# Attention, a transform and a channel-mixing layer on one core: three weight conversions in flight instead of two, and a weight block loaded earlier

## The chip, the cores and the metric

One core of one Trainium2 chip. The metric is the device time of one execution in microseconds; the figure shown is the median of three runs. A profiled execution is a run of its own, and its trace has a span from the first to the last instruction.

## The reference, cut to what matters

Four batches, eight heads, 1152 keys of 64 values; queries are averaged in pairs, which leaves 576 per head.

```
q_pool = q.reshape(B, H, S // 2, 2, D).mean(axis=3)
attn = softmax(q_pool @ k.T / sqrt(D));  x = attn @ v            # -> (4, 576, 512)
u = x + real(fft(fft(x, axis=1), axis=2))
un = (u - mean(u)) / sqrt(var(u) + 1e-6)
out = u + maximum(un @ w_ch1, 0) @ w_ch2                          # 512 -> 2048 -> 512
```

The two weight matrices come as 64-bit floats, and the kernel turns them into pairs of 32-bit floats (a high and a low part) on the chip.

## The kernel before, in words

**Attention.** The 32 heads are taken in 16 pairs, each in five units of query rows, 80 units in all. A unit has score matmuls (`s_piece`, L216) with a scaled copy and running minimum on DVE (L218), the exponential on ACT (L230), transposes on PE in `t_step` (L243) whose copies to SBUF go mostly to ACT (L246), and the product with the values in `av` (L259), whose result ACT copies into an output tile `x` (L263). Heads are loaded by SP and POOL's queue (L126, L127) and prepared on POOL (L185, L186, L192). The denominators go through DRAM (L279, L288) and are applied on POOL (L294).

**Per batch, beside attention.** When the four pairs of a batch are done, `mid` runs the transform (`dft`: folds on DVE, L490 and L498 on PE, additions on POOL, L503 and L504, and on DVE, L508) and the normalisation (`norm`: L522 to L590, with one matmul pair at L571). Then `ffn` does channel mixing in 32 blocks: 16 of the first matrix (`f1`: 12 matmuls, Relu on ACT at L697, the low part on DVE at L698) and 16 of the second (`f2`: 12 matmuls, an addition on DVE at L710), alternately four and four. A block needs one weight block of 512 KB, loaded by `wload` (L670) two blocks ahead into one of three buffers. Results go out at L712, from the same output tile that attention wrote.

**Conversions.** `convert` turns one raw weight block into its pair, 32 in all, numbered 0 to 31 here in the order of use, which is also that of the blocks of a batch (block 1 uses conversion 0). It loads the raw block on SP (L610, buffer `wraw`), takes an absolute value on ACT (L619), clamps and shifts on DVE (L621, L623), converts the low word on ACT (L625), merges on DVE (L629), masks on DVE (L632), copies on ACT (L636), does three steps on POOL (L637 to L639) and stores the pair to DRAM on SP (L645). `wraw` has two buffers; four tiles of the tag `cv` serve `wa`, `rest` and `wb` of all conversions in turn. The list `inside` lets one conversion at a time be between L619 and L639. Only batch 0 has to wait for conversions: its `ffn` steps past a block when the block two ahead has been stored.

**What sets the order.** There is no scheduler at work: the Python code writes every instruction down once, and each engine and queue runs its own in that order, waiting on semaphores. The code keeps a counter `now` in nanoseconds. Each step of attention adds a fixed amount, and what `convert` yields is how far `now` must come before its next step is written (the steps go through `after` and `run_events`). `conversions` starts a new one when `now` has reached `cdue` and fewer than two are running. `going` is filled when the first `ffn` begins. Between steps of attention `background` writes steps of `mid` and `ffn`. There are five output tiles; `drain`, called before unit 50 ends (the first unit of pair 10), writes steps of `ffn` of batch 0 until its block 30 is written, and no attention meanwhile, because that unit's result goes into batch 0's first tile.

Line numbers are those of the kernel before. Names in rows leave buffer numbers out.

Of the kernel before, what the change touches and what calls it, by code (L numbers as in the profile page):

```python
# [12 lines left out]
F32 = mybir.dt.float32  # L13
F32R = mybir.dt.float32r
I32 = mybir.dt.int32
# [9 lines left out]
P = 128  # L25
# [3 lines left out]
NH = HT + 1  # L29
# [25 lines left out]
def fused_kernel(ctx: ExitStack, tc: tile.TileContext, k2, q2, v2, w1, w2, cst, out):  # L55
# [10 lines left out]
    smp = pool("sm", 2)  # L66
    cvp = pool("cv", 1)
# [18 lines left out]
    def mtile(shape, dt, name):  # L86
        return mdp.tile(shape, dt, tag="mid", name=name)
# [4 lines left out]
    def ftile():  # L92
        return gtile() if tail[0] else ps_f.tile([P, 512], F32, tag="f", name="f")
# [322 lines left out]
    def dft(b):  # L416
# [3 lines left out]

        tmp = mtile([P, 2, SQ], F32, "tmp")
        last = smp.tile([1, SQ], F32, tag="last", name="last", bufs=1)
        z = smp.tile([1, NH], F32, tag="z", name="z", bufs=1)
        gap = 600 if b < B - 1 else 0
        nc.vector.tensor_copy(tmp[D:D + 1, 0, :], ua[:1, 1, :])
        nc.scalar.copy(last, ub[:1, 1, :])
# [178 lines left out]
    going = []  # L605

    def convert(f, which):
        src = (w1, w2)[which]
        w = cvp.tile([P, 512, 2], I32, tag="wraw", name="wraw", bufs=2)
        nc.sync.dma_start(w, src[f].bitcast(I32).rearrange("p (c x) -> p c x", x=2))  # L610
        yield 4000 if going else 7000
        while inside:
            yield 400
        inside.append(f)
        high, low = w[:, :, 1], w[:, :, 0]
        a = cvp.tile([P, 512], F32, tag="cv", name="wa", bufs=4)
        ai = a.bitcast(I32)

        nc.scalar.activation(a, high.bitcast(F32), AF.Abs)  # L619
        yield 1400  # L620
        nc.vector.tensor_scalar(a, a, WORD_MIN, WORD_MAX, op0=ALU.max, op1=ALU.min)  # L621
        yield 1000
        nc.vector.tensor_scalar(ai, ai, 3, 0x3FFFFFF8, op0=ALU.logical_shift_left, op1=ALU.bitwise_and)  # L623
        rest = cvp.tile([P, 512], F32, tag="cv", name="rest", bufs=4)
        nc.scalar.activation(rest, low.bitcast(U32), AF.Copy, scale=2.0 ** -52)  # L625
        yield 1000
        t = cvp.tile([P, 512], F32, tag="cv", name="wb", bufs=4)
        b = t.bitcast(I32)
        nc.vector.scalar_tensor_tensor(b, high, -0x40000000, ai, op0=ALU.bitwise_and, op1=ALU.bitwise_or)  # L629

        yield 1000
        nc.vector.tensor_scalar(ai, b, -0x800000, None, op0=ALU.bitwise_and)  # L632
        yield 1000
        h = w.rearrange("p c x -> p (c x)").rearrange("p (x c) -> p x c", x=2)
        hi, lo = h[:, 0, :], h[:, 1, :]
        nc.scalar.copy(hi.bitcast(F32R), t)  # L636
        nc.gpsimd.tensor_tensor(rest, rest, a, op=ALU.mult)  # L637
        nc.gpsimd.tensor_tensor(t, t, hi.bitcast(F32), op=ALU.subtract)
        nc.gpsimd.tensor_tensor(lo.bitcast(F32R), t, rest, op=ALU.add)  # L639
        if not going:  # L640
            yield 3000
        inside.pop()
        yield 3000 if going else 1500
        d = scw.tile([P, 2, 512], F32, name=f"w{which}_{f}")
        nc.sync.dma_start(d, h.bitcast(F32))  # L645
        wsc[which, f] = d
# [4 lines left out]
    todo = deque(ORDER)  # L651
    busy = []

    def converter():

        w, f = todo.popleft()
        g = convert(f, w)
        busy.append(f)

        def go():  # L660
            c = next(g, None)
            if c is not None:
                after(c, go)
            else:
                busy.pop()
        go()

    def wload(which, f, nm):
        w = wp.tile([P, 2, 512], F32R, tag="w", name=nm)
        nc.sync.dma_start(w.bitcast(F32), wsc[which, f])  # L670
        return w
# [5 lines left out]
    def mm3(ps, ah, al, bh, bl, first, last):  # L677
        nc.tensor.matmul(ps, lhsT=ah, rhs=bh, start=first, stop=False)  # L678
        nc.tensor.matmul(ps, lhsT=al, rhs=bh, start=False, stop=False)  # L679
        nc.tensor.matmul(ps, lhsT=ah, rhs=bl, start=False, stop=last)  # L680

    def ffn(b):
        gs = {}
        hl = u = None

        n_tok = NT if b < B - 1 else NL

        def f1(f, t, w):
            src = (gp, "g") if t == 0 else (kv, "ks")
            g = gs[f, t] = src[0].tile([P, 2, n_tok], F32R, tag=src[1], name="g" if b < B - 1 else "g3")  # L690
            w = w.rearrange("p x (j c) -> p x j c", j=4)
            hi, lo = hl[t]
            ps = ftile()[:, :n_tok]
            for j in range(4):
                mm3(ps, w[:, 0, j, :], w[:, 1, j, :], hi[j // 2][:, j % 2, :n_tok], lo[j // 2][:, j % 2, :n_tok],
                    j == 0, j == 3)
            nc.scalar.activation(g[:, 0, :], ps, AF.Relu)  # L697
            after(1000, lambda: nc.vector.scalar_tensor_tensor(g[:, 1, :], ps, 0.0, g[:, 0, :].bitcast(F32),  # L698
                                                               op0=ALU.max, op1=ALU.subtract))

        def f2(q, m, t, w):
            w = w.rearrange("p x (i c) -> p x i c", i=GF)
            ps = ftile()[:, :n_tok]
            for i in range(GF):
                g = gs[q * GF + i, t]
                mm3(ps, w[:, 0, i, :], w[:, 1, i, :], g[:, 0, :], g[:, 1, :], i == 0, i == GF - 1)
            x = u[m // 2][:, m % 2, :]
            last = q == NFC // GF - 1
            if b < B - 1:
                nc.vector.tensor_tensor(x[:, :NT], ps, x[:, :NT], op=ALU.add)  # L710
                if last:
                    after(2500, lambda: nc.sync.dma_start(out[b, m, :, :NT], x[:, :NT]))  # L712
                return
            c = slice(t * HT, t * HT + HT)
            r = rest[:, m, t * 96:t * 96 + 96]
            nc.vector.tensor_tensor(x[:, c], ps[:, :HT], x[:, c], op=ALU.add)
            nc.vector.tensor_tensor(r, ps[:, HT:], r, op=ALU.add)
            if last:
                nc.sync.dma_start(out[b, m, :, c], x[:, c])
                if t:  # L720
                    nc.sync.dma_start(out[:B - 1, m, :, NT:].rearrange("b p c -> p b c"),
                                      rest[:, m].rearrange("p (b c) -> p b c", b=B - 1))

        blocks = [(q, which, i) for q in range(NFC // GF) for which in range(2) for i in range(GF)]

        def load(n):
            at = b + n // len(blocks), n % len(blocks)
            if at[0] < B and at not in loads:
                q, which, i = blocks[at[1]]
                loads[at] = wload(which, q * GF + i, f"w{which + 1}")  # L730

        for n, (q, which, i) in enumerate(blocks):
            while b == 0 and n + 2 < len(blocks) and (blocks[n + 2][1], blocks[n + 2][0] * GF + blocks[n + 2][2]) not in wsc:
                yield 0
            if n == 0:
                load(0)
                load(1)
                yield 0
                while b not in ready:
                    yield 0  # L740
                going.append(b)
                hl = un.pop(b)
                u = ut.pop(b)
                if b == B - 1:
                    rest = mtile([P, 4, 3 * D], F32, "rest3")
                    nc.sync.dma_start(rest, left[2])
            load(n + 2)
            w = loads.pop((b, n))
            for t in range(len(hl)):
                if which == 0:  # L750
                    f1(q * GF + i, t, w)
                else:
                    f2(q, i, t, w)
                if q == NFC // GF - 1 and t == len(hl) - 1:
                    if which == 0 and i == GF - 1:
                        done_f1.add(b)
                    if which == 1:
                        done_f2.add((b, i))
                yield 2720 if b < B - 1 else 2080

    def mid(b):
        yield 0, 1000
        yield from dft(b)
        yield 0, 3500
        yield from norm(b)
        yield 0, 4500
        ready.append(b)

    now = due = credit = 0.0
    cdue = 60000.0  # L770
# [6 lines left out]
    def after(wait, fn):  # L777

        heapq.heappush(events, (now + wait, next(tick), fn))
# [55 lines left out]

    def conversions():
        nonlocal cdue
        if now >= cdue and todo and len(busy) < 2:
            converter()
            cdue = now + (5500 if going else 10000 if nb == 0 else 8500)  # L840

    nb = 0
    for pe in attention():
# [72 lines left out]
```

## Time and profile before

| | before |
|---|---|
| median of 3 runs | 1078.88 us (1074.13 to 1081.51) |
| profiled execution, its span | 1081.19 us, 1079.4 us |
| PE busy, PE weight loads | 984.8 us (91%), 853.7 us (79%) |
| DVE, ACT, POOL busy | 630.8 (58%), 525.1 (49%), 372.7 us (35%) |
| DMA | 170.89 MB, mean 158 GB/s |
| mean granted clock of PE | 0.968 |
| chain that ended last | PE 59%, DVE 8%, DMA 5%, issue 3%, ACT 3% |

The span is what the trace covers; the profiled execution's own time is 1.8 us longer. PE overlaps weight loads with matmuls, so its busy time is not all work at its peak; idle time of PE, and the granted clock of a stretch (1.00 is 2.4 GHz, 0.50 is 1.2 GHz), are read from stretches.

### The profile page before, as it was taken

The page shows a single profiled execution, that of the slowest core. Times are in us where ns is not written, and L with a number is a line of the kernel's source. Part 1 is how long each engine was busy: PE and PEld are TensorE (multiplying, and loading weights), DVE is VectorE, ACT ScalarE, POOL GpSimd, SP SyncE. Part 2 cuts the span into 40 slices and gives each one's busy share as a digit, 9 for nine tenths or more (in the row PEclk, how much of TensorE's full clock was granted, in tenths as well). Part 3 has the DMA queues.
Part 4 walks back from the last instruction along what each step waited for, and adds up shares of the span by engine and source line. Part 5 has one row for each costly group of instructions (what it writes and reads, how often), then busy time and mean ns, then how long its engine had stood idle before and what let it go on. Part 6 is the DMA issues. An engine that isn't in the chain of part 4 may idle for free.

```text
span 1079.4 us, 19451 instructions
## 1 busy us (share of the span) xinstructions
PE 984.8 (91%) x7392; PEld 853.7 (79%) x7392; DVE 630.8 (58%) x1518; ACT 525.1 (49%) x1017; POOL 372.7 (35%) x351
## 2 busy tenths in 40 slices
PE   6999998988799899994599999989899989999998
PEld 5898876767688777773488888878688867899998
DVE  5556879798576597986435457475544254522222
ACT  5678876667455466674144445455444421311100
POOL 3545666665355456664322222252200002000000
PEclk9999999999899899997799999999999999999999
DMA  5545656544566665645536355234532243634344
GB/s 180 168 133 168 201 158 207 176 130 152 163 228 228 213 210 175 203 165 180 192 131 190 129 176 137 82 107 144 164 124 91 92 153 117 216 142 135 118 127 127
DMA packets 62512, 170.89 MB, mean 158 GB/s; under 512 B 16770, under 2 KB 20242, under 8 KB 62420
## 3 DMA queue, kind: packets, MB, share of 16 engines
q1 hardware_dynamic: 58100, 151.96, 44.1%
q0 software_dynamic: 4320, 17.70, 5.2%
q8 instruction: 58, 0.95, 0.4%
q14 instruction: 34, 0.28, 0.1%
HBM read 146.88 MB, written 22.75 MB: 157 GB/s over the span
## 4 chain that ended last, share of the span: by engine, by line
PE 59%; DVE 8%; DMA 5%; issue 3%; ACT 3%; POOL 1%; SPq 0%; DVEq 0%; ACTq 0%; POOLq 0%
PE o L259 8%; PE f L678 8%; PE f L680 7%; PE s L216 7%; PE f L679 7%; PE t L243 6%; PE t L678 4%; PE t L680 4%; PE t L679 4%; DVE sp L218 2%; DMA wraw<-in_w 2%; PE f L498 1%; DMA w<-wraw 1%; DMA w<-w 1%; ACT pt L246 1%
## 5 line engine op out<-in xcount | busy, mean ns | idle before, releaser
L218 DVE TENSOR_SCALAR_CACHE_REDUCE sp<-s,bia 128x384 f32<-128x384 f32 x288 | 177.3, 616 | 81.7 <-PE s L216 60.3
L216 PE MATMUL s<-ks,qh 128*128 128x384 f32 x480 | 186.3, 388 | 26.3 <-ACT pt L246 16.7
L259 PE MATMUL o<-pt,vs 128*64 128x128 f32 (+1 forms) x2880 | 173.3, 274 | 12.0 <-DVE pt L246 7.7
L259 PEld LDWEIGHTS o<-pt,vs 128*64 128x64 f32 x2880 | 152.7, 142 | 36.9 <-issue 21.3
L230 ACT ACTIVATE sp<-sp,bia 128x1152 f32<-128x1152 f32 x144 | 180.3, 1257 | 1.2 <-DVE sp L218 1.1
L246 ACT COPY pt<-t 128x512 f32<-128x512 f32 (+2 forms) x243 | 124.3, 527 | 103.1 <-PE t L243 101.8
L216 PE MATMUL s<-ks,ql 128*128 128x384 f32 x480 | 165.6, 345 | 0.4 <-POOL ql L165 0.4
L243 PE MATMUL t<-ident,sp 128*128 128x128 f32 x1045 | 150.4, 277 | 10.7 <-DVE sp L218 7.3
L243 PEld LDWEIGHTS t<-ident,sp 128*128 128x128 f32 x1045 | 122.1, 141 | 30.7 <-DVE sp L218 12.6
L216 PEld LDWEIGHTS s<-ks,qh 128*128 128x128 f32 x480 | 92.7, 193 | 38.3 <-ACT pt L246 21.5
L698 DVE SCALAR_TENSOR_TENSOR g<-f,g 128x512 fp32r<-128x512 f32 (+1 forms) x52 | 34.7, 668 | 116.4 <-ACT g L697 116.3
L216 PEld LDWEIGHTS s<-ks,ql 128*128 128x128 f32 x480 | 93.6, 195 | 1.3 <-POOL ql L165 0.8
L186 POOL TENSOR_TENSOR ks<-kr,ks 64x1152 fp32r<-64x1152 f32 x30 | 82.0, 2732 | 29.8 <-DMA kr<-in_k 9.2
L637 POOL TENSOR_TENSOR rest<-rest,wa 128x512 f32<-128x512 f32 x32 | 43.0, 1343 | 139.5 <-DVE wa L632 108.7
L678 PE MATMUL f<-unh,w 128*128 128x512 f32 (+1 forms) x208 | 83.6, 402 | 8.2 <-DMA w<-w 8.2
L697 ACT ACTIVATE g<-f 128x512 fp32r<-128x512 f32 (+1 forms) x52 | 30.1, 580 | 124.4 <-PE f L680 124.4
L218 DVE TENSOR_SCALAR_CACHE_REDUCE sp<-s 128x384 f32<-128x384 f32 x144 | 78.7, 547 | 19.4 <-PE s L216 17.6
L192 POOL TENSOR_TENSOR ql<-qr,qh 128x576 fp32r<-128x576 f32 (+2 forms) x45 | 49.9, 1123 | 95.9 <-ACT qh L191 89.2
L680 PE MATMUL f<-unl,w 128*128 128x512 f32 (+1 forms) x208 | 81.3, 391 | 0.0
L679 PE MATMUL f<-unh,w 128*128 128x512 f32 (+1 forms) x208 | 81.1, 390 | 0.0
L678 PE MATMUL f<-g,w 128*128 128x512 f32 (+1 forms) x188 | 75.0, 399 | 2.1 <-DVE g L698 0.9
L185 POOL TENSOR_TENSOR qr<-qr 128x576 f32<-128x576 f32 x30 | 43.2, 1441 | 96.2 <-DMA qr<-in_q 96.2
(149 smaller groups left out, 1780.4 us busy)
## 6 DMA issues: line engine op xcount, KB each, us to landing
w<-w SPq DMA_DIRECT2D x128, 512.0 KB
qr<-in_q SPq DMA_DIRECT2D x30, 576.0 KB
ks<-in_k POOLq DMA_DIRECT2D x30, 576.0 KB, 5.6
wraw<-in_w SPq DMA_DIRECT2D x32, 512.0 KB
w<-wraw SPq DMA_DIRECT2D x32, 512.0 KB
vs<-in_v SPq DMA_DIRECT2D x32, 288.0 KB
kr<-in_k SPq DMA_DIRECT2D x30, 288.0 KB
out<-x SPq DMA_DIRECT2D x12, 256.0 KB
```

The lines of the kernel that those rows point to most:

```text
L185: nc.gpsimd.tensor_tensor(qr[:, 0, :], qr[:, 0, :], qr[:, 1, :], op=ALU.add)
L186: nc.gpsimd.tensor_tensor(ks[D:, :], kr[D:, :], ks[D:, :].bitcast(F32), op=ALU.subtract)
L192: nc.gpsimd.tensor_tensor(ql[:, c:c + b - a], qr[:, 0, a:b], qh[:, c:c + b - a].bitcast(F32), op=ALU.subtract)
L216: nc.tensor.matmul(ps, lhsT=l, rhs=k, start=i == 0, stop=i == len(ops) - 1)
L218: nc.vector.tensor_scalar(sp[n, j][:, c], ps, -0.0625, bt[:, pc - 1:pc] if pc else None, op0=ALU.mult, op1=ALU.min, accum_out=bt[:, pc:pc ...
L230: last_exp[0] = nc.scalar.activation(t, t, AF.Exp, bias=bia.pop((n, j))[:, 2:3], scale=-1.0, accum_out=den[pr][:, col:col + 1]).ins
L243: nc.tensor.transpose(ps[:, i * P:i * P + P], sp[k][:, c * P:(c + 1) * P], ident)
L246: (nc.vector.tensor_copy if eng == "v" else nc.scalar.copy)(pt[:, :o], ps[:, :o])
L259: nc.tensor.matmul(po[y * D:y * D + D, :w], lhsT=qkv[2 * pr + y][3][:, c, :], rhs=pt[:, o:o + w], start=c == 0, stop=c == NKC - 1)
L678: nc.tensor.matmul(ps, lhsT=ah, rhs=bh, start=first, stop=False)
L679: nc.tensor.matmul(ps, lhsT=al, rhs=bh, start=False, stop=False)
L680: nc.tensor.matmul(ps, lhsT=ah, rhs=bl, start=False, stop=last)
```

## The change

A third buffer for raw blocks, with up to three conversions running, shorter waits between the steps of a conversion once channel mixing has begun, and a new one started after 4600 counted nanoseconds there instead of 5500. The third weight block of a batch is loaded together with the first two. The transform's row `z` moves into an unused row of `tmp`; that gives room in SBUF.

```diff
-        z = smp.tile([1, NH], F32, tag="z", name="z", bufs=1)
+        z = tmp[:1, 0, :NH]
...
-        w = cvp.tile([P, 512, 2], I32, tag="wraw", name="wraw", bufs=2)
+        w = cvp.tile([P, 512, 2], I32, tag="wraw", name="wraw", bufs=3)
...
         nc.scalar.activation(a, high.bitcast(F32), AF.Abs)
-        yield 1400
+        yield 900 if going else 1400
         nc.vector.tensor_scalar(a, a, WORD_MIN, WORD_MAX, op0=ALU.max, op1=ALU.min)
-        yield 1000
+        yield 700 if going else 1000
         nc.vector.tensor_scalar(ai, ai, 3, 0x3FFFFFF8, op0=ALU.logical_shift_left, op1=ALU.bitwise_and)
...
         nc.scalar.activation(rest, low.bitcast(U32), AF.Copy, scale=2.0 ** -52)
-        yield 1000
+        yield 700 if going else 1000
...
-        yield 1000
+        yield 700 if going else 1000
         nc.vector.tensor_scalar(ai, b, -0x800000, None, op0=ALU.bitwise_and)
-        yield 1000
+        yield 700 if going else 1000
...
                 load(0)
                 load(1)
+                load(2)
                 yield 0
...
-        if now >= cdue and todo and len(busy) < 2:
+        if now >= cdue and todo and len(busy) < 3:
             converter()
-            cdue = now + (5500 if going else 10000 if nb == 0 else 8500)
+            cdue = now + (4600 if going else 10000 if nb == 0 else 8500)
```

In the rows below, `w_2_1817` and its like on the right of an arrow are the stored pairs in DRAM (the first number is the block of its matrix), and `w_3668` on the left is a buffer that a block is loaded into. SP's queue in unit 35, where the first blocks of batch 0 begin, before:

```order
L127 DMA vs<-in_v 128x576
L670 DMA w_3668<-w_2_1817 128x1024
L670 DMA w_3690<-w_3_1992 128x1024
L279 DMA rd<-rs 9x128
L645 DMA w_4_3732<-wraw 128x1024
```

Now, some 40 rows earlier, where the first loads stand:

```order
L670 DMA w_2272<-w_0_1430 128x1024
L670 DMA w_2274<-w_1_1621 128x1024
L670 DMA w_2276<-w_2_1819 128x1024
L610 DMA wraw<-in_w 128x1024
L645 DMA w_1_2413<-wraw 128x1024
```

And at the place in unit 35:

```order
L127 DMA vs<-in_v 128x576
L670 DMA w_3691<-w_3_1994 128x1024
L279 DMA rd<-rs 9x128
L645 DMA w_5_3733<-wraw 128x1024
L610 DMA wraw<-in_w 128x1024
```

The third block's load has moved from behind the values of a head to the other two; the fourth block's alone is left, and the store behind it is one conversion further.

SP's queue at the end of the drain, units 50 and 51, before (`w_13` to `w_15` are the last conversions, 29 to 31):

```order
L645 DMA w_13_5982<-wraw 128x1024
L670 DMA w_5984<-w_13_5982 128x1024
L610 DMA wraw<-in_w 128x1024
L645 DMA w_14_6041<-wraw 128x1024
L670 DMA w_6043<-w_14_6041 128x1024
L598 DMA left<-unh 128x2x64 x2
L598 DMA left<-unl 128x2x64 x2
L598 DMA left<-x 128x2x64 x2
L712 DMA out<-x 128x512
L645 DMA w_15_6073<-wraw 128x1024
L670 DMA w_6075<-w_15_6073 128x1024
L712 DMA out<-x 128x512
```

And now:

```order
L288 DMA r<-rd 64x576
L288 DMA r<-rd 64x512
L288 DMA r<-rd 64x64
L670 DMA w_5977<-w_13_5728 128x1024
L645 DMA w_15_5994<-wraw 128x1024
L670 DMA w_6038<-w_14_5836 128x1024
L712 DMA out<-x 128x512
L670 DMA w_6059<-w_15_5994 128x1024
L712 DMA out<-x 128x512
```

Of the stores of conversions one is left here, no raw load is, and the two stores of results stand ahead of `left`.

DVE in unit 45, behind the transform's additions, before:

```order
L511 TENSOR_TENSOR x<-last,f 1x287
L218 TENSOR_SCALAR sp,bia<-s,bia 128x384 x2
L246 COPY pt<-t 128x512
L621 TENSOR_SCALAR wa<-wa 128x512
L218 TENSOR_SCALAR sp,bia<-s 128x384
L218 TENSOR_SCALAR sp,bia<-s,bia 128x384
L623 TENSOR_SCALAR wa<-wa 128x512
L522 TENSOR_TENSOR lsum<-x 128x576
L218 TENSOR_SCALAR sp,bia<-s,bia 128x384
L218 TENSOR_SCALAR sp,bia<-s 128x384
L629 SCALAR_TENSOR_TENSOR wb<-wraw,wa 128x512
```

And now:

```order
L621 TENSOR_SCALAR wa<-wa 128x512
L508 TENSOR_TENSOR x<-x,f 128x289
L508 TENSOR_TENSOR x<-x,f 128x287
L508 TENSOR_TENSOR x<-x,f 128x289
L508 TENSOR_TENSOR x<-x,f 128x287
L623 TENSOR_SCALAR wa<-wa 128x512
L510 TENSOR_TENSOR x<-last,f 1x289
L511 TENSOR_TENSOR x<-last,f 1x287
L629 SCALAR_TENSOR_TENSOR wb<-wraw,wa 128x512
L218 TENSOR_SCALAR sp,bia<-s,bia 128x384 x2
```

Two steps of a conversion stand among the additions, and its merge at L629 stands ahead of the two score pieces that were next.

## Rows read from the trace of the kernel before

**Rows 1.** Windows: stretch, length, busy us of each engine, granted clock, DMA share.

```profile
core 0: us, PE busy (x) PEld busy (x) DVE busy (x) ACT busy (x) POOL busy (x), PEclk, DMA share, GB/s
287.00:545.00 258.00, 212.52 (x1513) 176.90 (x1512) 174.76 (x366) 131.62 (x251) 137.76 (x117) 0.91 0.61 199
293.00:486.00 193.00, 180.64 (x1330) 152.03 (x1331) 142.89 (x311) 111.50 (x214) 111.22 (x97) 0.96 0.61 202
408.00:448.00 40.00, 36.98 (x295) 29.64 (x295) 32.12 (x74) 25.97 (x54) 29.66 (x27) 1.00 0.60 186
486.00:545.00 59.00, 31.52 (x182) 24.72 (x181) 30.50 (x51) 19.96 (x36) 26.54 (x20) 0.74 0.55 183
```

**Rows 2.** Waits of PE from 287 to 545 us: in total, times, longest.

```profile
PE s L216 <- ACT pt L246: 12.7, 1, 12.7
PE f L571 <- DVE g L698: 12.6, 2, 6.6
```

**Rows 3.** Timeline from 278 to 299 us: start, duration, engine, line [idle before <- releaser].

```profile
278.95 0.40 PE L678 MATMUL f<-unh,w 128*128 128x512 f32 x1
...
281.72 0.27 PE L272 MATMUL t<-ident,den 128*9 128x128 f32 x1
...
286.36 1.28 SPq L670 DMA_DIRECT2D w<-w  x2
...
292.88 0.77 PE L678 MATMUL f<-unh,w 128*128 128x512 f32 x1 [5.64 <-DMA w<-w]
...
298.14 0.66 PE L243 MATMUL t<-ident,sp 128*128 128x128 f32 x4
```

**Rows 4.** Timeline from 358 to 372 us.

```profile
358.47 0.35 SPq L610 DMA_DIRECT2D wraw<-in_w  x1
...
366.32 0.66 ACT L619 ACTIVATE wa<-wraw 128x512 f32<-128x512 f32 x1 [6.56 <-DMA wraw<-in_w]
...
367.51 4.10 PE L259 MATMUL o<-pt,vs 128*64 128x128 f32 x34 [3.92 <-ACT pt L246]
```

**Rows 5.** Waits of the SP queue, and one of ACT, from 287 to 545 us.

```profile
SPq L610 <- DMA w<-wraw: 39.3, 12, 6.8
...
SPq L670 <- DMA w<-wraw: 25.0, 7, 5.8
...
ACT wa L619 <- DMA wraw<-in_w: 21.2, 6, 6.6
```

**Rows 6.** Timeline from 519 to 545 us, the end of the drain.

```profile
519.96 2.19 PE L259 MATMUL o<-pt,vs 128*64 128x128 f32 x36
...
526.93 0.36 SPq L645 DMA_DIRECT2D w<-wraw  x1
...
533.52 0.38 SPq L712 DMA_DIRECT2D out<-x  x1
...
538.15 0.27 ACT L263 COPY x<-o 128x128 f32<-128x128 f32 x1 [15.44 <-DMA out<-x]
...
538.95 0.69 PE L216 MATMUL s<-ks,qh 128*128 128x384 f32 x1 [12.74 <-ACT pt L246]
...
540.53 3.87 PE L259 MATMUL o<-pt,vs 128*64 128x128 f32 x36
```

**Rows 7.** Lines of DVE from 287 to 545 us, the conversion's four steps.

```profile
L621 DVE TENSOR_SCALAR wa<-wa 128x512 f32<-128x512 f32 x18 | 18.5, 1030 | 15.7 <-ACT wa L619 15.7
L623 DVE TENSOR_SCALAR wa<-wa 128x512 int32<-128x512 int32 x19 | 17.1, 900 | 0.3
...
L629 DVE SCALAR_TENSOR_TENSOR wb<-wraw,wa 128x512 int32<-128x512 int32 x19 | 16.2, 855 | 1.3 <-POOL wraw L639 1.2
...
L632 DVE TENSOR_SCALAR wa<-wb 128x512 int32<-128x512 int32 x19 | 8.0, 421 | 0.0
```

**Rows 8.** Lines of POOL from 287 to 545 us: first step of a conversion.

```profile
L637 POOL TENSOR_TENSOR rest<-rest,wa 128x512 f32<-128x512 f32 x19 | 26.1, 1373 | 91.1 <-DVE wa L632 69.3 <-ACT wraw L636 10.4 <-ACT y L491 7.2
```

**Rows 9.** Line 621 in the whole span: duration ns, lowest, median, highest.

```profile
L621 DVE TENSOR_SCALAR wa<-wa x32: 412/998/2929, 91.0 to 518.8; 128x512 f32<-128x512 f32 x32
```

## The prediction

> **What bounds the kernel now.** I read the page's 40 slices first: PE is at 9 tenths or more in most of them, with one hole in slices 19 and 20. So the question is where PE stands idle, and I asked the windows from the first channel-mixing blocks to the point behind the hole. From 287 to 545 us PE is busy 212.5 of 258 us [rows 1], 45.5 us idle. Of this 27.5 us lie in 486 to 545, where the granted clock is also down to 0.74. The chain of waits and the timeline then name four causes.
>
> First, the third weight block. PE stands 5.64 us before the third block of batch 0, for a load issued at 286.36 [rows 3]. Behind the wait PE runs at the lower of its two clocks: the block takes 298.14 − 292.88 = 5.26 us, where the first block took 281.72 − 278.95 = 2.77 [rows 3].
>
> Second, a raw weight block that comes late. ACT's absolute value stands 6.56 us for it; it was issued at 358.47 and used at 366.32. ACT is in order, so the copies of transposed scores queue behind it, and PE waits 3.92 us; the attention-value group then takes 4.10 us [rows 4], against 2.19 for a full one [rows 6]. ACT waits so six times, 21.2 us [rows 5].
>
> Third, the drain. Attention of head pair 10 needs an output tile of batch 0, so block 30 of batch 0 must be done first, and that needs its weights converted. Weights are late: SP stands 25.0 us in loads of blocks whose store has just been issued, and 39.3 us in raw loads that need the buffer of such a store [rows 5]. PE waits twice, 12.6 us, for a PSUM buffer [rows 2], because DVE and ACT sit in order behind conversion steps.
>
> Fourth, the end of the drain: ACT waits 15.44 us to overwrite the output tile, whose second store is issued at 533.52, behind the last conversion's store at 526.93 and the load that follows it; PE waits 12.74 us for ACT [rows 6].
>
> **The change part by part.** The span is 1079.4 us, the profiled execution 1081.19, 1.8 us more, and the median of the runs 1078.88, 2.3 us less than that. I sum against the span. From block 31 on, the rows of all engines stand almost as before, so what is gained or lost by then should remain.
>
> *The third block ahead.* Its load moves from row 119 of SP's order to right behind the first two, long before it is needed. The wait of 5.64 and the slow block's excess, 5.26 − 2.77 = 2.49, can go: 8.1. The load that then stands first in that place is the fourth block's; before, it was the second of a pair issued by 287.6 and did not hold PE. I take 8; bounds 0 and 8.1.
>
> *A third raw buffer.* A raw load now reuses the buffer of the store three conversions back, not two, so most of SP's 39.3 us should go, and the block lies ready when ACT comes to it. The case at 358 costs PE 3.92 + (4.10 − 34/36 × 2.19 = 2.03) = 5.95. I take 6; bounds 0 and 6.
>
> *Three in flight and closer steps.* In the order, conversions 12 to 26 are stored in units 34 to 49 before, 12 to 30 now; the last is stored in unit 50 ahead of block 29's matmuls, where five were left for unit 50 and beyond. So the drain has blocks 27 to 30 to compute and hardly a conversion to wait for. What can be had: the 27.5 us idle, and the lower clock. For that, the last attention-value group shows 3.87 − 2.19 = 1.7 [rows 6]; two more stalls of 6 us stand in the window [rows 2], so I take three times 1.7, about 5. Together 32.5.
>
> What stays of it: the output tile. Issue of the second store to ACT's copy is 538.15 − 533.52 = 4.6 us, and DVE's addition before it is short. PE worked from 519.96 to 538.95 − 12.74 = 526.2, 6.2 us, before it stood. Now the last load ahead of that store waits for a conversion long stored, so the store should go some 1 to 3 us behind block 30. That leaves 0 to 4 us idle; I take 2.5 with the clock. Other small waits among loads and PSUM buffers: 4. So 32.5 − 6.5 = 26; bounds 11 (the output tile's 12.7 stays, with its clock and the small waits) and 32.5.
>
> *What the denser conversions cost.* The conversions that were in the drain now lie beside attention, the transform and the normalisation of batch 1. One takes of DVE 1.030 + 0.900 + 0.855 + 0.421 = 3.2 us [rows 7], and of POOL three steps like the one of 1.373 [rows 8], about 4.1. Four or five more in 293 to 486 are 13 to 16 us on DVE, which has 193 − 142.9 = 50 us free there [rows 1]. On the average that fits. In the stretch 408 to 448 (units 44 to 46) it does not fit well: DVE is busy 32.1 and POOL 29.7 of 40 [rows 1], and the order now has two more conversions there, 6.4 and 8.2 us, which brings both to 38 of 40. The place is the additions of the transform, where two conversion steps now stand between them, and line 629 stands right behind with the next pieces of scores queued after it. Line 629 needs a buffer that POOL's last step of the conversion before frees; it waited once, 1.2 us [rows 7]. The price is bounded by 0 and by all of 16 us of DVE. I take 7, of which 5 are here.
>
> DVE's conversion steps are longer beside POOL: line 621 takes 412 ns at the least, 998 in the median and 2929 at most [rows 9], so a mean over a stretch with more POOL in it may rise. The Trainium skill (SBUF — State Buffer, "Who interferes with whom") says that such DVE operations and GpSimd's exclude each other for a whole instruction. By it, each of some 20 conversions could find one more POOL step in its way, an estimate of 1.4 us each from rows 8, 27 us of DVE time in all; the sum does not use it.
>
> *The transform's z row in a row of tmp.* DVE's writer and ACT's reader keep their places, and tmp's slot is next taken by the transform's y1, which ACT writes after that read on its own queue. I take 0; if the order of ACT did not cover it, it would be one row copy of under a microsecond in each of four batches.
>
> *Sum.* 8 + 6 + 26 − 7 = 33. The span becomes 1046.4, the execution 1048.2, and at the level of the median 1045.9: **1046**.
>
> **The rivals.**
> 1. *DVE locked to POOL's pace (slower).* Place: line 629, in order ahead of the score pieces; cv still has four tiles and a conversion takes three. With closer steps the next conversion comes to line 629 while POOL is still at the one before. For: two POOL steps of 1.37 can be left when it comes, and unit 45's order. Against: one wait in 19 conversions now [rows 7], and a spacing in the order that is still wide outside units 44 to 46. Price: up to 4.1 us in each of some 20 conversions. It decides from 40/20 = 2 us each, which eats the 40 us of gains; at 2.5 us it gives 1079 + 10 = 1089. The rule of the Trainium skill cited above (SBUF — State Buffer) would push this way; rows 9 agree with its direction.
> 2. *The output tile takes over the drain's end.* The second store stays behind something on SP, or DVE's addition is late, and PE still stands some 12.7 us there [rows 6]. For: this wait is the longest of all and does not need a conversion to exist. Against: what held the store was the last conversion. The gain of the drain falls to 11: 8 + 6 + 11 − 7 = 18, so 1061.
> 3. *The conversions fit.* DVE's free 50 us [rows 1] take them, and the drain leaves nothing: 8 + 6 + 32.5 = 46.5, so 1032.
> 4. *The change does not speed conversions.* One conversion at a time is between its first and last step, so three in flight may only wait longer. Against: the order stores four more before the drain. Time: 1079 less the 8 of the third block, 1071.
>
> **How the numbers follow.** Forecast 0.64, rival 2 0.15, rival 3 0.13, rival 4 0.04, rival 1 0.04. The range runs from 1031, just under rival 3, to 1064, which takes in rival 2; outside are rivals 1 and 4 and the tails of the others. A measurement of this kernel can tell about 1% from no change, that is 10.8 us: slower is rival 1, 0.04; within 1% are rival 4 and a hundredth of rival 2, 0.05; faster is the rest, 0.91.
>
> **What would show it.** Right: no wait of PE for a weight load before the third block; ACT's waits for raw blocks under 5 us in total; SP's waits in raw loads under 10; the stretch from unit 50's start to the end of unit 51 some 25 us shorter, with PE's wait for ACT there under 4 us; in units 44 to 46 new waits of DVE at line 629 of a few microseconds, and some 5 us more on PE. Wrong: a wait of over 10 us of ACT for the output tile (rival 2); waits at line 629 adding to more than 40 us (rival 1); idle time of PE before the drain that grows by more than 15 us; or stretches behind block 31 that last longer than before.

## The result, and the profile after

| | before | after |
|---|---|---|
| median of 4 runs, in the same session | 1078.53 us (1074.13 to 1081.51) | 1052.22 us (1050.72 to 1053.36) |
| profiled execution, its span | 1081.19, 1079.4 us | 1051.75, 1050.0 us |
| PE, DVE, ACT, POOL busy | 984.8, 630.8, 525.1, 372.7 us | 975.2, 635.5, 524.7, 371.7 us |
| mean granted clock of PE | 0.968 | 0.980 |

The ratio is 0.9758, 95% interval [0.9722, 0.9795]: 26.3 us faster, where I forecast 33 (1046.0). The result lies inside the range, 6 us above the forecast, and that small difference hides several terms that were off in opposite directions.

To see where, I take from each trace the start of every attention-value group (36 matmuls at L259; 80 groups, numbered from 0, one per unit). "The start of unit n" in the expectations below is the start of group n; what the prediction calls unit n runs from group n−1 to group n. A row is the time of the kernel before; the other columns are later (+) or earlier (−) than that, in us.

| group | before | changed | e1 | e2 | e3 | e4 | e5 | e6 | e7 | e8 |
|---|---|---|---|---|---|---|---|---|---|---|
| 34 | 284.7 | +2.7 | −2.4 | +1.1 | +1.8 | +3.5 | −2.3 | −0.8 | −8.6 | +3.5 |
| 35 | 304.0 | −5.5 | −10.3 | +0.7 | +1.3 | −4.8 | −10.6 | −9.2 | −16.9 | −4.2 |
| 36 | 316.5 | −0.1 | −5.2 | +0.8 | +2.1 | −3.1 | −8.2 | −9.2 | −14.4 | −2.9 |
| 40 | 363.2 | −0.8 | −5.2 | +0.6 | +3.8 | +0.1 | −6.3 | −9.3 | −13.6 | +3.3 |
| 41 | 382.2 | −1.1 | −8.1 | −6.5 | +1.3 | −6.5 | −8.1 | −16.4 | −16.2 | −3.3 |
| 46 | 447.1 | +12.5 | −8.2 | −4.6 | +5.9 | +7.0 | −3.6 | −14.6 | −11.4 | +2.7 |
| 49 | 479.6 | +11.5 | −6.6 | −3.6 | +7.8 | +10.8 | −1.5 | −13.6 | −13.3 | +3.6 |
| 52 | 554.8 | −24.6 | −6.6 | −15.7 | −18.8 | −25.2 | −29.1 | −26.0 | −50.6 | −31.8 |
| 79 | 856.8 | −27.4 | −9.5 | −18.6 | −19.6 | −26.7 | −31.6 | −28.8 | −53.7 | −32.4 |

Each column is one profiled execution, and a level can be off by some 3 us: e9 and e10, the same program as e4 up to group 34, stand there at +3.5 and −0.2. So I read differences inside a column, not levels, and no cause is claimed for the +2.7 at group 34. Differences are not exact either: e4 and e8, one program up to group 40, lose 3.2 and 6.2 us from group 36 to 40. And a traced execution can lie off the median of its kernel: e4's by +4.9 us, e8's by +6.0, e5's by −3.2, e6's by −3.7.

The changed column reads: 8.2 us gained before group 35, 5.4 given straight back by group 36, 1.0 gained from 36 to 41, 12.6 lost from 41 to 49, and 36.1 gained from 49 to 52, the drain. The region of [rows 1], moved to where the same work lies now, then groups 41 to 49, the transform of batch 1 within them, and the drain:

```profile
core 0: us, PE busy (x) PEld busy (x) DVE busy (x) ACT busy (x) POOL busy (x), PEclk, DMA share, GB/s
287.00:520.00 233.00, 209.93 (x1555) 177.34 (x1554) 176.91 (x365) 132.29 (x252) 136.69 (x117) 0.95 0.67 215
...
382.00:491.00 109.00, 95.67 (x695) 80.28 (x690) 94.13 (x184) 63.29 (x124) 70.14 (x59) 0.94 0.59 192
422.00:470.00 48.00, 40.39 (x285) 32.82 (x285) 39.85 (x73) 24.73 (x48) 36.54 (x33) 0.89 0.59 189
491.00:531.00 40.00, 37.69 (x295) 32.31 (x295) 26.96 (x67) 23.09 (x44) 17.81 (x16) 1.00 0.74 222
```

PE's idle time in the region fell from 45.5 us [rows 1] to 23.1 (233 − 209.9). The drain, last line, is now busy for 37.7 of 40 us at full clock. Of what is left, 13.3 us lie between groups 41 and 49, and 7.6 of these around the transform of batch 1 (422 to 470), at clock 0.89, with DVE busy 39.9 of 48 and POOL 36.5.

The waits of the changed kernel from 287 to 531 us (in total, times, longest), of PE and ACT, then of the SP queue, against [rows 2, 5]:

```profile
ACT wa L619 <- DMA wraw<-in_w: 13.1, 3, 6.2
...
ACT x L263 <- DMA out<-x: 7.9, 1, 7.9
...
PE t L243 <- DVE sp L218: 5.8, 2, 3.7
...
PE o L259 <- ACT pt L246: 3.9, 2, 3.6
...
PE s L216 <- DVE sp L218: 3.6, 2, 2.0
```

```profile
SPq L610 <- DMA w<-wraw: 59.1, 17, 7.0
```

No wait of PE for a weight load of over half a microsecond is left, nor the two waits for a PSUM buffer behind L698. PE's longest waits are now for DVE's score pieces at L218. The third raw buffer has not freed SP: 39.3 us [rows 5] became 59.1. And the wait near 366 us has stayed (timeline), against [rows 4]:

```profile
347.20 0.33 SPq L610 DMA_DIRECT2D wraw<-in_w  x1
...
361.47 0.33 SPq L610 DMA_DIRECT2D wraw<-in_w  x1
...
365.12 0.66 ACT L619 ACTIVATE wa<-wraw 128x512 f32<-128x512 f32 x1 [6.17 <-DMA wraw<-in_w]
...
365.51 2.62 POOL L186 TENSOR_TENSOR ks<-kr,ks 64x1152 fp32r<-64x1152 f32 x1
...
365.81 2.60 DVE L621 TENSOR_SCALAR wa<-wa 128x512 f32<-128x512 f32 x1 [3.61 <-ACT wa L619]
366.30 3.70 PEld L259 LDWEIGHTS o<-pt,vs 128*64 128x64 f32 x34 [3.80 <-ACT pt L246]
366.30 4.10 PE L259 MATMUL o<-pt,vs 128*64 128x128 f32 x34 [3.55 <-ACT pt L246]
```

Counted through, the block that ACT waits for is the one asked for at 361.47, 3.65 us before; the one asked for at 347.20 was still waiting for its turn. The order of the two engines, with buffer numbers, says why (SP's raw loads, then ACT's first step, of the changed kernel):

```
L610 DMA wraw_4339<-in_w2 128x1024
L610 DMA wraw_4475<-in_w2 128x1024
...
L619 ACTIVATE wa_4529<-wraw_4475 128x512
L619 ACTIVATE wa_4640<-wraw_4339 128x512
```

With three in flight two conversions wait for `inside` to become empty; each looks every 400 counted nanoseconds, and whichever looks first goes. The block just loaded overtook the one that had waited.

### The profile page after: what moved, and what is told of

It reads as the page before. It is cut to its first block, busy times and chain, and to the rows that moved or that the text cites. A ratio compares the mean times of both kernels' runs of the same rounds, so it can differ in the third digit from the quotient of the medians.

```text
span 1050.0 us, 19452 instructions
## 1 busy us (share of the span) xinstructions
PE 975.2 (93%) x7392; PEld 849.0 (81%) x7392; DVE 635.5 (61%) x1518; ACT 524.7 (50%) x1017; POOL 371.7 (35%) x351
## 4 chain that ended last, share of the span: by engine, by line
PE 50%; DVE 4%; ACT 1%; DMA 1%; issue 1%; SPq 0%; DVEq 0%; ACTq 0%
PE f L678 6%; PE f L680 6%; PE f L679 6%; PE s L216 6%; PE o L259 5%; PE t L243 5%; PE t L678 4%; PE t L680 4%; PE t L679 4%; DVE sp L218 1%; PE f L498 1%; DMA out<-x 1%; PE t L498 0%; DVE dg L561 0%; DVE x L710 0%
## 5 line engine op out<-in xcount | busy, mean ns | idle before, releaser
L218 DVE TENSOR_SCALAR_CACHE_REDUCE sp<-s,bia 128x384 f32<-128x384 f32 x288 | 177.2, 615 | 78.9 <-PE s L216 56.5
L259 PE MATMUL o<-pt,vs 128*64 128x128 f32 (+1 forms) x2880 | 171.1, 272 | 13.8 <-DVE pt L246 9.6
L259 PEld LDWEIGHTS o<-pt,vs 128*64 128x64 f32 x2880 | 150.6, 141 | 37.7 <-issue 20.7
L246 ACT COPY pt<-t 128x512 f32<-128x512 f32 (+2 forms) x243 | 125.2, 527 | 107.6 <-PE t L243 102.9
L698 DVE SCALAR_TENSOR_TENSOR g<-f,g 128x512 fp32r<-128x512 f32 (+1 forms) x52 | 34.7, 667 | 101.8 <-ACT g L697 101.8
L186 POOL TENSOR_TENSOR ks<-kr,ks 64x1152 fp32r<-64x1152 f32 x30 | 82.3, 2744 | 29.7 <-DMA kr<-in_k 11.3
L678 PE MATMUL f<-unh,w 128*128 128x512 f32 (+1 forms) x208 | 82.3, 396 | 0.0
L218 DVE TENSOR_SCALAR_CACHE_REDUCE sp<-s 128x384 f32<-128x384 f32 x144 | 78.5, 545 | 5.6 <-PE s L216 4.3
L679 PE MATMUL f<-unh,w 128*128 128x512 f32 (+1 forms) x208 | 79.7, 383 | 0.0
```

The lines of the kernel that those rows point to most:

```text
L186: nc.gpsimd.tensor_tensor(ks[D:, :], kr[D:, :], ks[D:, :].bitcast(F32), op=ALU.subtract)
L218: nc.vector.tensor_scalar(sp[n, j][:, c], ps, -0.0625, bt[:, pc - 1:pc] if pc else None, op0=ALU.mult, op1=ALU.min, accum_out=bt[:, pc:pc ...
L246: (nc.vector.tensor_copy if eng == "v" else nc.scalar.copy)(pt[:, :o], ps[:, :o])
L259: nc.tensor.matmul(po[y * D:y * D + D, :w], lhsT=qkv[2 * pr + y][3][:, c, :], rhs=pt[:, o:o + w], start=c == 0, stop=c == NKC - 1)
```

## The experiments

Gains in microseconds are worked out from the ratio to the kernel before, which ran again in each session (medians 1077.82 for e1 to e4, 1077.29 for e5 to e8, 1075.36 for e9 to e12).

**The parts alone.** e1 changes this in the kernel before, and nothing else:

```diff
                 load(0)
                 load(1)
+                load(2)
```

> The kernel before with only the third weight block loaded ahead of its place. Theory: PE's wait of 5.64 us before the third block and the slow block behind it go, so unit 35 starts about 8 us earlier; here the conversions are as sparse as before, so the gain is not given straight back in units 35 and 36 as in the changed kernel, and most of it lasts to the end: 1071 to 1074 us. Rival: whatever lies in units 35 and 36 on DVE and POOL takes it back also with sparse conversions, or the drain's end is set by the conversions and swallows it: 1077 to 1080 us.

Measured: 1069.57 us, ratio 0.9922 [0.9894, 0.9951], 8.4 us. Before group 35, 7.9 us are gained, the size of the term; 5.1 of it go by group 36, 2.9 come back by group 41, and the drain passes the rest on nearly unchanged. From group 34 to 52 that leaves 4.2 us in the column (−2.4 to −6.6); where the rest of the 8.4 comes from is not shown. So gain is given back without the closer steps too, against my theory. But e1's reason is another than the changed kernel's (below), and e6, which has the third block and the old steps, gives nothing back (−9.2 at groups 35 and 36).

e2, in the kernel before (with z in tmp, which makes the room):

```diff
-        w = cvp.tile([P, 512, 2], I32, tag="wraw", name="wraw", bufs=2)
+        w = cvp.tile([P, 512, 2], I32, tag="wraw", name="wraw", bufs=3)
...
-        if now >= cdue and todo and len(busy) < 2:
+        if now >= cdue and todo and len(busy) < 3:
```

> The kernel before with three conversions in flight and three raw buffers (and z in a row of tmp), steps and spacing as before, no third block ahead. Theory: since only one conversion at a time stands between its first and last step, the third in flight mostly waits for its turn; the drain shortens a little, 1068 to 1078 us. Rival, the prediction's: the third in flight and the third buffer carry the change; the raw-block wait of 6 us goes and the drain loses 20 us or more, 1048 to 1060 us.

Measured: 1060.51 us, 0.9833 [0.9801, 0.9866], 18 us. My theory of that moment falls. Conversions do overtake here too, but with the old steps the leads are long enough: ACT waits for no raw block at all, and the 7.1 us between groups 40 and 41 are gained, just as the prediction's term for the third buffer had it. The drain (49 to 52) gives 12.1, less than the 20 of the rival.

e3, in the kernel before (and the other three waits of 1000 likewise):

```diff
-        yield 1400
+        yield 900 if going else 1400
...
-        yield 1000
+        yield 700 if going else 1000
...
-            cdue = now + (5500 if going else 10000 if nb == 0 else 8500)
+            cdue = now + (4600 if going else 10000 if nb == 0 else 8500)
```

> The kernel before with only the closer steps and the spacing of 4600 once channel mixing has begun; two in flight, two raw buffers, z in its own tile, no third block ahead. Theory: the order stores the conversions almost where the changed kernel does, so the drain (start of unit 50 to start of unit 52) falls from 34.8 to about 22 us and the time is 1050 to 1060 us. Rival: with two buffers each raw load stands behind the store just issued, ACT's waits for raw blocks grow over 35 us and hold PE, 1065 us or more.

Measured: 1059.07 us, 0.9828 [0.9798, 0.9857], 18.5 us. The drain gives 26.6 us, and 6.5 are lost from 41 to 49. Two buffers do not hold it up: ACT's raw waits fall to 15.7 us.

**Two parts together.** e5 is e3 with e1's line, so the changed kernel without e2's edit; e6 is e2 with e1's line, so the changed kernel without e3's.

```diff
 # to e3 and to e2 alike
+                load(2)
```

> The changed kernel with two conversions in flight and two raw buffers again (closer steps, spacing 4600 and the third block ahead stay; z in its own tile). Theory: with closer steps the third in flight adds little, since one conversion at a time sets the pace; the gains of the closer steps (19 us alone) and of the third block (8 us alone) add in part, 1048 to 1054 us, as the changed kernel. Rival: the third in flight and its buffer are needed as they were with the old steps (17 us alone): 1058 us or more.

> The changed kernel with the old steps and the old spacing of 5500 (three in flight, three raw buffers and the third block ahead stay). Theory: what stays of the drain is set by the pace of the conversions, so the drain from unit 49 to unit 52 still holds some 15 to 20 us that the closer steps take away, but the units before it are not slowed: raw-block waits none, unit 49 starts 10 us or more earlier than before, and the time is 1050 to 1056 us. Rival: the third block's 8 us is swallowed by the drain, which waits for the same conversions: 1058 to 1062 us.

Measured: e5 1053.49 us, 0.9782 [0.9745, 0.9819]; e6 1054.02 us, 0.9769 [0.9738, 0.98]. Both are the changed kernel's ratio within the intervals. The single gains are 8.4, 18 and 18.5, together 44.9; the third block adds to either of the others (5 us to closer steps, within the intervals, and 7 to three in flight, beyond them), but three in flight and closer steps have one gain between them. The table shows how: e6 reaches group 49 at −13.6, where the changed kernel is at +11.5, 25.1 us apart: 3.7 by group 35, 5.4 more from 35 to 36, 6.8 from 40 to 41 (the late raw block), 9.8 from 41 to 49. In the drain e6 then gains 12.4 and the changed kernel 36.1. What the closer steps save in the drain, they have cost before it. e6 still stands once in the drain:

```profile
494.09 0.79 PE L678 MATMUL f<-g,w 128*128 128x512 f32 x1 [12.33 <-DVE g L698]
```

**The turn.** e4 is the changed kernel with

```diff
-    inside = []
+    inside, turns = [], []
...
-        src = (w1, w2)[which]
+        src = (w1, w2)[which]; turns.append(f)
...
-        while inside:
+        while inside or turns[0] != f:
             yield 400
-        inside.append(f)
+        inside.append(turns.pop(0))
```

> The changed kernel, with waiting conversions taken up in the order in which their raw blocks were loaded. Theory: the raw-block wait stayed because a block just loaded overtook one that had waited longer; in turn, ACT's waits for raw blocks fall from 13.1 to under 5 us, the wait of PE near 366 us (3.55 us and the long group behind it) goes, and the time is 1045 to 1049 us. Rival: the block is late because its buffer comes free late, whatever the turn; ACT's waits stay at 10 us or more and the time at 1050 to 1054 us.

Measured: 1049.03 us, 0.9734 [0.9707, 0.9762]. ACT's raw waits are gone, and 6.6 us between groups 40 and 41 are gained, so overtaking was the cause of the late block. On the whole time it is worth about 2.6 us, which the intervals do not tell from nothing: from 41 to 49 e4 loses 17.3 us where the changed kernel lost 12.6, in a trace that is 4.9 us above e4's median, so how much of that loss the other executions have is not known.

**What is lost from group 41 to 49.** e7, in the changed kernel, and e12, in the kernel before:

```diff
-        nc.gpsimd.tensor_tensor(rest, rest, a, op=ALU.mult)
-        nc.gpsimd.tensor_tensor(t, t, hi.bitcast(F32), op=ALU.subtract)
+        nc.gpsimd.tensor_tensor(rest[:, :32], rest[:, :32], a[:, :32], op=ALU.mult)
+        nc.gpsimd.tensor_tensor(t[:, :32], t[:, :32], hi[:, :32].bitcast(F32), op=ALU.subtract)
```

> The changed kernel in which two of POOL's three steps of each conversion work on 32 of 512 columns (the product with the power of two and the subtraction of the high part; the low parts of the weights are then not those of the reference). Theory: what the denser conversions cost in units 41 to 49 (12 us) comes from DVE steps that stretch beside POOL; DVE's conversion steps get shorter, the cost falls by 5 us or more, and the time is 1040 to 1047 us. Rival: it is DVE's own work in a full queue, or the order; DVE's steps shorten by little and the time stays at 1049 to 1053 us.

> The kernel before with the same two of POOL's steps of each conversion on 32 of 512 columns (the low parts of the weights are then not those of the reference). Theory: POOL beside DVE hurts above all where conversions are dense, so here it is worth less than the 26 us by which it shortened the changed kernel: units 41 to 49 gain at most 4 us, and the whole 8 to 18 us (1059 to 1069 us). Rival: POOL's steps cost the same per conversion wherever they lie: 24 us or more, 1054 us or less.

Measured: e7 1025.97 us, 0.9516 [0.9488, 0.9544], 26 us less than the changed kernel; e12 1057.4 us, 0.9818 [0.978, 0.9855], 19.6 us less than before; e7 gains more and e12 a little more than I had expected. Ahead of group 34, e7 has gained 11.3 us on the changed kernel and e12 9.2 on the kernel before. From 41 to 49, e7 loses 2.9 us where the changed kernel lost 12.6; e12 gains 2.9. So POOL's steps are dear everywhere, and in this stretch 9.7 us with the denser conversions against 2.9 without. The edit also makes the conversion shorter, which these two runs do not separate. The stretch from group 41 to 49 before, and in e7 (the changed kernel's stands above, 382 to 491):

```profile
382.20:479.60 97.40, 90.22 (x696) 75.69 (x695) 83.63 (x179) 59.88 (x117) 58.52 (x52) 0.98 0.57 185
```

```profile
366.00:466.30 100.30, 92.82 (x708) 78.21 (x707) 84.21 (x187) 64.21 (x125) 46.76 (x59) 0.98 0.63 208
```

PE is idle for 7.2 us before, 13.3 in the changed kernel and 7.5 in e7, at a granted clock of 0.98, 0.94 and 0.98. If I add up what each of DVE's four conversion steps took over the least of its line, that comes to 7.2 us before (32 instructions), 15.9 in the changed kernel (40) and 7.9 in e7 (39). DVE's merge in the stretch from 382 to 491 us, changed kernel and then e7:

```profile
L629 DVE SCALAR_TENSOR_TENSOR wb<-wraw,wa 128x512 int32<-128x512 int32 x10 | 13.0, 1302 | 1.2 <-POOL wraw L639 1.2
```

```profile
L629 DVE SCALAR_TENSOR_TENSOR wb<-wraw,wa 128x512 int32<-128x512 int32 x9 | 6.3, 705 | 0.1
```

The price is not in waits at L629 (1.2 us) but in its duration. How it reaches PE, in the changed kernel's timeline:

```profile
446.33 3.02 POOL L186 TENSOR_TENSOR ks<-kr,ks 64x1152 fp32r<-64x1152 f32 x1
...
447.81 2.10 DVE L629 SCALAR_TENSOR_TENSOR wb<-wraw,wa 128x512 int32<-128x512 int32 x1
...
449.44 1.74 POOL L192 TENSOR_TENSOR ql<-qr,qh 128x576 fp32r<-128x576 f32 x1
449.83 1.96 DVE L522 TENSOR_TENSOR lsum<-x 128x576 f32<-128x576 f32 x1
...
451.71 0.60 DVE L218 TENSOR_SCALAR_CACHE_REDUCE sp<-s,bia 128x384 f32<-128x384 f32 x1
...
452.38 1.14 PEld L243 LDWEIGHTS t<-ident,sp 128*128 128x128 f32 x6 [3.96 <-DVE sp L218]
452.38 1.54 PE L243 MATMUL t<-ident,sp 128*128 128x128 f32 x6 [3.73 <-DVE sp L218]
```

A merge of 0.69 us (median) takes 2.10 behind POOL's head preparation, an addition of the normalisation (0.74 at the least) 1.96 behind the next, the score piece queued after them starts at 451.71, and PE stands 3.73 us and works at the lower clock behind it (0.50 granted from 452.38 to 456).

e8 adds to e4 that ACT makes DVE's copy of transposed scores in seven units; e11 adds the same to e6.

```diff
-                yield tr(x, "v" if j < 4 and y == 1 else "a")
+                yield tr(x, "v" if j < 4 and y == 1 and not 41 <= i < 50 else "a")
```

> The changed kernel with conversions taken up in the order of their loads, and the one copy of transposed scores per unit that DVE makes given to ACT in units 41 to 49. Theory: DVE's queue bounds these units (24 to 27 of 30 us busy, ACT 18), so with 5 us of copies less on DVE the units from 41 to 49 take 4 to 8 us less and the time is 1041 to 1046 us. Rival: ACT is in order with more than copies, and what DVE gives up ACT holds back: 1047 to 1054 us.

> The changed kernel with the old steps and spacing throughout, and the copy of transposed scores given to ACT in units 41 to 49 (no turns). Theory: with old steps DVE is not the limit in these units, so the copies are worth little there (0 to 4 us), and the 12 us that PE stands in the drain stay: 1048 to 1054 us. Rival: DVE's queue is the limit with old steps too and shortens the drain as well: 1046 us or less.

Measured: e8 1040.7 us, 0.9656 [0.9612, 0.97]; e11 1053.61 us, 0.9796 [0.9763, 0.983]. Beside e4 (0.9734) e8 gains 8 us, and from 41 to 49 it loses 6.9 us instead of 17.3. Beside e6 (0.9769) e11 gains nothing. So the same edit paid where conversions are close and not where they are wide, which fits DVE's queue as the limit there; e8 also keeps turns and e11 does not, a difference that no run takes apart. e8 is the fastest version with the whole computation here, 37 us below before and 11 below the changed kernel.

**Closer steps late.** e9 adds this to e8, for conversions 24 to 31 (and the other three waits of 700 likewise; the spacing of 4600 stays); e10 has 20 in place of 24.

```diff
+        n = f // 4 * 8 + which * 4 + f % 4
+        quick = n >= 24
...
-        yield 900 if going else 1400
+        yield 900 if quick else 1400
...
-        yield 700 if going else 1000
+        yield 700 if quick else 1000
```

> The changed kernel with conversions taken up in turn, the copy of transposed scores given to ACT in units 41 to 49, and the closer steps only for the last eight conversions (24 to 31). Theory: the closer steps cost their 12 us in units 41 to 49, beside POOL and the transform, and pay only in the drain; used late, unit 49 starts 12 us or more earlier than before, the drain (unit 49 to unit 52) still falls by 24 us or more, and the time is 1032 to 1041 us. Rival: with old steps up to unit 45 the last conversions come too late, as with old steps throughout; the drain falls by 16 us or less and the time is 1046 to 1054 us.

> As the run before it in this call, with the closer steps from conversion 20 on (unit 41). Theory: three stores then lie in unit 45, beside the transform, where DVE and POOL are full, so units 41 to 49 lose 4 to 8 us more than in the run before, and the drain gains 0 to 4 us more: 1036 to 1045 us. Rival: the drain decides, and the sooner the conversions are done the better: below the run before by 3 us or more.

Measured: e9 1055.63 us, 0.9805 [0.9771, 0.984]; e10 1044.97 us, 0.9724 [0.968, 0.9769]. Of my theory the first half held: e9 goes from −10.3 at group 41 to −4.7 at 49, 16.2 us ahead of the changed kernel. The second fell: the drain then gives only 19.2, between the theory's 24 and the rival's 16, and the time is past the rival's 1054. PE stands in the drain 7.3 us for a PSUM buffer and 4.6 for ACT (waits of PE from 470 to 525 us; lines behind `convert` are two higher here):

```profile
PE f L680 <- DVE x L712: 7.3, 1, 7.3
PE s L216 <- ACT pt L246: 4.6, 1, 4.6
```

e10 loses 4.7 us more than e9 from 41 to 49, as I had expected, but its drain gives 29.1 (−4.3 to −33.4), 9.9 more, and it ends 10.7 us below e9: the rival's sign. In this kernel a saving before the drain did not replace conversions that are done before it.

## Why the prediction was right or wrong

**Third block ahead, 8.** Right in size: 8.2 us from group 34 to 35, and 7.9 in e1. In the changed kernel 5.4 are given back in the next unit. The step that failed is what is late next: the prediction asked only after the fourth block's load, which held nothing, and not after the fifth block's, nor after DVE. In the changed kernel the fifth block's load holds PE for 0.37 us at 301.65, and DVE does the rest: its steps lie beside POOL's head preparation, the score pieces come behind them, and PE waits and then has a granted clock of 0.55 (310.5 to 314.3):

```profile
306.30 2.97 POOL L186 TENSOR_TENSOR ks<-kr,ks 64x1152 fp32r<-64x1152 f32 x1
...
307.30 2.26 DVE L632 TENSOR_SCALAR wa<-wb 128x512 int32<-128x512 int32 x1
...
310.14 0.66 PE L243 MATMUL t<-ident,sp 128*128 128x128 f32 x4 [2.05 <-DVE sp L218]
```

In e1 the fifth block's load comes first: PE waits 2.01 us for it, the granted clock behind that is 0.50 (299.4 to 302.6), and only then a shift on DVE lasts as long as POOL's step and holds the score pieces.

```profile
297.85 0.50 PE L678 MATMUL f<-g,w 128*128 128x512 f32 x1 [2.01 <-DMA w<-w]
...
302.56 2.65 POOL L186 TENSOR_TENSOR ks<-kr,ks 64x1152 fp32r<-64x1152 f32 x1
...
302.86 2.63 DVE L623 TENSOR_SCALAR wa<-wa 128x512 int32<-128x512 int32 x1
...
306.08 0.44 PE L216 MATMUL s<-ks,qh 128*128 128x384 f32 x1 [1.67 <-DVE sp L218]
```

**Third raw buffer, 6.** Nothing came of it (0.3 us from group 40 to 41). The step that failed is "the block lies ready when ACT comes to it". With the closer steps the third buffer gave no lead, because the conversions were not taken up in turn: e4, with turns, has the term (6.6), and e2, with wide steps and no turns, has it too (7.1). ACT's waits for raw blocks, which I expected under 5 us, were 13.1. SP's waits at L610, which I expected under 10, rose to 59.1: that a raw load need not wait for a store was wrong as well, since a new conversion starts when one has ended, so its load still stands behind a store just issued.

**The drain, 26.** Mis-sized: 36.1 from group 49 to 52, of which 2.7 is block 26 (12 matmuls at full clock, one every 0.23 us), which now lies ahead of group 49; 33.4 is left. The upper bound, 32.5, was the better value. Of the 6.5 us that I left as residue little stayed: ACT's wait for the output tile fell from 15.44 to 7.9 us, and PE's, 12.74 [rows 6], to this:

```profile
516.06 0.93 PE L243 MATMUL t<-ident,sp 128*128 128x128 f32 x6 [1.62 <-ACT pt L246]
```

**Denser conversions, −7.** Mis-sized: 12.6 from group 41 to 49, less block 26's 2.7, is 9.9, and with the 5.4 behind group 35 it is 15.3, at the end of the bounds (0 to 16). The place was right, units 44 to 46: from group 44 (+1.8) to 46 (+12.5) 10.7 us are lost. The mechanism is not a new wait at L629, as I wrote (1.2 us in all, as before), but steps of DVE that stretch beside POOL (15.9 us against 7.2 from group 41 to 49) and push back the score pieces; the prediction named that lengthening and left it out of the sum.

**The sum.** 8.2 + 0.3 + 33.4 − 9.9 − 5.4 = 26.6. The forecast, 33, was 6.4 above it: 5.7 too much for the buffer and 8.3 for the denser conversions, 7.4 too little for the drain. That the total came so near is in part luck, since these errors cancel. The rivals: 1 did not occur; 2 did not, the output tile costs PE 1.6 us; 3 had the drain right but not the cost; 4 (1071) is outside the interval. Behind group 52, 2.8 us more are gained in the profile, as in most columns, so they seem to belong to the profile of before, which is 2.7 us above its median.

**What the prediction could not show** is that three in flight and closer steps compete for the same gain. It summed them as one term, and e5 and e6 show that either alone, with the third block, reaches the same time.

## What to carry to other kernels

A gain that several edits reach by the same path (here: conversions done before the drain) is had once; ask of each edit what it still gives when the other is there, and what it costs on the way. Where several workers poll for one slot and leads are short, a deeper buffer may give nothing unless the slot is given in the order of loading. And a queue that is 80% busy in a stretch can be the next bound when its work is made denser: moving a copy of 0.68 us per unit off it was worth 8 us (e8 beside e4), where three in flight with the third buffer was not told from nothing beside e5.

## What the runs showed of the hardware

DVE's conversion steps read and write SBUF, and a POOL step holds them up whole. In the trace of the changed kernel L621, L623, L629 and L632 take 0.41 to 0.67 us at the least. All 37 of their 128 instructions that took over 0.25 us longer than their line's least end 0.28 to 0.55 us behind the end of a POOL step on tensors (36 of 36 before). Score pieces read PSUM, on the same engine in the same stretches, and never stretch (first line below: duration ns, lowest, median, highest). Nor do DVE's copies of transposed scores (L246, 64 of 671 to 693 ns) and its additions at L710 (48 of 677 to 694), which read PSUM too; the additions at L522, from SBUF to SBUF, do (744 to 2696).

```profile
L218 DVE TENSOR_SCALAR_CACHE_REDUCE sp<-s,bia x288: 598/617/622, 10.3 to 821.6; 128x384 f32<-128x384 f32 x144
```

```profile
L632 DVE TENSOR_SCALAR wa<-wb x32: 411/422/2519, 96.2 to 494.8; 128x512 int32<-128x512 int32 x32
```

This is the rule of the Trainium skill (SBUF — State Buffer, "Who interferes with whom") that whoever comes first holds the shared ports for a whole instruction, and the traces agree where POOL comes first. The estimate that I drew from it, one more POOL step for each conversion, they do not bear out: the stretch of all these steps from 287 to 531 us is 24.0 us before and 27.9 after (75 and 76 instructions), and over the whole span 41.0 and 40.3. The costliest partner is none of POOL's conversion steps but the head preparation at L186 (up to 3.2 us each, 11.0 of the 27.9).
